# Loading the first 512 rows of x in four quarters on two queues, and moving the gate row's product to another PSUM bank

## The chip, the core and the metric

The kernel runs on one core of one Trainium2 chip. The metric is the device time of one execution in microseconds (us), as the median of several executions. All executions told here are of the fast state, except where the text says otherwise. Every execution also has a profile span (first to last instruction), about 1.3 us shorter than its time; a position in a trace is counted in us from the start of that span.

Words used below: SBUF and PSUM are the two memories in which this kernel keeps its tiles. In it TensorE writes its products to banks of PSUM (`PS<-` in the views), and DVE (the vector engine) or ACT (the scalar engine) copies them to SBUF (`XT<-PS`). SP and ACT issue the DMA transfers; a transfer "lands" at the moment that the profile gives as its landing (in before, the second half at 3.66 us, and the transpose that waited for it started at 3.71). The "pitch" is the time from the start of one matmul to the start of the next, and the "switch" the moment at which it goes from about 0.427 to 0.216 us for 512 columns. The texts call it the clock switch, and the slow pitch a slow clock; but the granted clock reads 1.00 in before from 0 to 5 us, at the slow pitch, so only the spacing of matmuls shows the switch.

## The reference, cut to what matters

```python
x = A_x                                              # 1 x 2048 x 512, bf16
g = sigmoid((x * gate_w).sum(-1, keepdims=True))     # one gate per row
a = linear_attention(x, A_wqkv, A_w_phi, A_wo)       # 32 heads of 16, two softmaxes as feature map
b = relu(x @ B_w1) @ B_w2                            # 512 -> 1376 -> 512
return g * a + (1 - g) * b
```

Only the opening concerns us: in this kernel the first 512 rows of x ("x0") are brought into SBUF with the 512 features on the partitions before `x @ w1` begins, and gate_w becomes one more column of w1.

## The kernel before: the parts that matter

All rows but the first 512 are transposed by the DMA. x0 is loaded plainly, as two halves on one queue (SP), and transposed by TensorE, 16 blocks of 128 x 128 multiplied by an identity. A block is named (dt, j): feature block dt, and j, the quarter of x0 whose rows it holds. Until x0 has landed, TensorE does filler matmuls.

```python
def loadx0(h):
    p.dma("sp", lambda e: e.dma_start(out=XS[:, 2*h:2*h+2, :], in_=xq[:, 2*h:2*h+2, :]), f"x0{h}", ev=f"x0{h}")
...
A, B = (0, 1), (2, 3)          # quarters of the first and of the second half
warm(5)                        # five fillers of 512 columns
p.early("pe")
warm(1, 384)                   # and one of 384
xtr("a0", A, (0,), 6)          # name, quarters, feature blocks, PSUM bank
xtr("a1", A, (1,), 5)
xtr("a2", A, (2,), 7, last=False)
xtr("c0", (2,), (0,), 2)       # the second half is waited for here
xtr("d0", (3,), (0,), 0)
xtr("a2", A, (3,), 7, off=2 * P)
xev("dve", "a0", A, (0,), 6)   # xev: copy from PSUM to SBUF, on DVE or ACT
xev("act", "c0", (2,), (0,), 2)
xev("dve", "d0", (3,), (0,), 0)
...
xtr("b1", B, (1, 2), 1)
xtr("b3", B, (3,), 6)
...
slab(0)                        # 8 products x0[feature block 0] @ w1; needs a0, c0, d0 and w1's first piece
```

"Slab t" is eight matmuls of 512 columns with the t-th feature block; after slab 3 come two more products, and then the gate row and two value tiles:

```python
hunit(0, 8)                    # banks 3 and 4
hunit(0, 9, "dve")
gatecol(3 + rot[0] % 3)        # bank 5: gate_w transposed by a 4-column matmul, copied into w1 by DVE
vtile(0, "dve")                # bank 2
vtile(1, "act", nextbank())    # bank 5 again
for i in range(4):
    pre(i)                     # banks 0, 1, 6, 7
```

The softmax here doesn't subtract the row's maximum and nothing guards it: scores larger than these inputs give would overflow.

## Time and profile before

| | before |
|---|---|
| median of the first three executions | 147.24 us (147.05 to 147.31) |
| the execution that was profiled | 147.74 us, span 146.4 us |
| TensorE busy | 143.2 us, 98% of the span |
| fillers, x0's transposes, slab 0 begin at | 0.39, 2.94, 4.75 us |

The lines behind this stand in the prediction. Lines of the timeline and of the chain begin with start and length in us; L numbers are lines of that kernel, so the same operation moves by one or two lines between kernels (transposes L239 before, L237 after; slabs L522 and L520; value tiles L406 and L404). A name such as `OT<-in_A_x_dram` is the load of x0 (its buffer shares memory with OT), and `PS<-ONE` a filler.

### The profile page before, as it was taken

What the parts mean: (1) busy time and instruction counts of PE and PEld (TensorE: products, weight loads), DVE (VectorE), ACT (ScalarE), POOL (GpSimd) and SP (SyncE); (2) the same over time, 40 slices, a digit from 0 to 9 for tenths busy, and PEclk for the clock granted to TensorE, in tenths of its full rate; (3) what the DMA queues carried; (4) which work ended last, traced back from release to release, by engine and by line L of the source; (5) the groups of instructions that cost most, each with busy time, mean ns of one, the idle gap of its engine ahead of it and who ended that gap; (6) DMA issues with size and microseconds to landing.
All of it is one profiled execution on the core that took longest, in us unless ns stands there. A gap on an engine that the chain in (4) does not pass through costs nothing.

```text
span 146.4 us, 2522 instructions
## 1 busy us (share of the span) xinstructions
PE 143.2 (98%) x961; PEld 73.4 (50%) x978; DVE 92.5 (63%) x158; ACT 72.8 (50%) x125; POOL 52.2 (36%) x62
## 2 busy tenths in 40 slices
PE   8999999999999999999999999999999999999994
PEld 3544664444445545545644555554444444444443
DVE  3517737777688878678698977674445555555342
ACT  3307467897778778887878862022221111111150
POOL 2040002778768678687869820300000000000000
DMA  6999993033449975335743431454243222322213
GB/s 201 283 272 206 221 182 68 0 71 72 76 85 336 149 213 76 72 72 107 44 106 74 105 72 29 83 108 116 68 100 79 72 72 57 91 72 74 72 44 106
DMA packets 45221, 16.12 MB, mean 110 GB/s; under 512 B 39352, under 2 KB 44568, under 8 KB 45208
## 3 DMA queue, kind: packets, MB, share of 16 engines
q1 hardware_dynamic: 45056, 15.92, 49.7%
q8 instruction: 8, 0.13, 0.4%
q10 hardware_dynamic: 152, 0.03, 0.1%
q14 instruction: 5, 0.04, 0.1%
HBM read 4.41 MB, written 2.10 MB: 44 GB/s over the span
## 4 chain that ended last, share of the span: by engine, by line
PE 97%; issue 1%; DVE 1%; DVEq 0%
PE PS L485 25%; PE PS L274 19%; PE PS L330 18%; PE PS L494 9%; PE PS L406 9%; PE PS L522 5%; PE PS L460 3%; PE PS L428 3%; PE PS L286 2%; PE PS L232 2%; PE PS L239 1%; PE PS L308 1%; DVE WQK L508 1%; DVE ONE L208 0%; DVEq L655 0%
## 5 line engine op out<-in xcount | busy, mean ns | idle before, releaser
L485 PE MATMUL PS<-W,HT 128*128 128x512 bf16 (+3 forms) x182 | 40.2, 366 | 0.3
L374 POOL TENSOR_TENSOR EB<-EB,SC 128x1024 bf16<-128x1024 bf16 x15 | 28.9, 1930 | 24.7 <-DVE SC L372 24.7
L350 ACT ACTIVATE EB<-PS 128x480 bf16<-128x480 f32 (+1 forms) x44 | 30.1, 756 | 14.2 <-PE PS L330 14.2
L499 ACT ACTIVATE TFA<-PS,GT 128x512 bf16<-128x512 f32 x16 | 11.0, 687 | 42.7 <-PE PS L494 36.6
L274 PE MATMUL PS<-XT,W 128*128 128x512 bf16 x124 | 30.2, 379 | 0.2
L330 PE MATMUL PS<-WQK,XT 128*128 128x480 bf16 x128 | 28.5, 366 | 0.0
L370 DVE TENSOR_REDUCE ZB<-EB 128x64 f32<-128x1024 bf16 x15 | 18.3, 1220 | 14.2 <-ACT EB L350 14.2
L508 DVE SCALAR_TENSOR_TENSOR WQK<-PS,OMG,TFA 128x512 bf16<-128x512 f32 (+2 forms) x17 | 12.2, 719 | 23.6 <-ACT TFA L499 22.4
L485 PEld LDWEIGHTS PS<-W,HT 128*128 128x128 bf16 (+1 forms) x187 | 17.0, 98 | 17.4
L260 ACT ACTIVATE HT<-PS 128x512 bf16<-128x512 f32 x35 | 20.3, 614 | 7.5 <-PE PS L522 5.6
L330 PEld LDWEIGHTS PS<-WQK,XT 128*128 128x128 bf16 x128 | 12.5, 98 | 13.6
L385 DVE TENSOR_REDUCE ZB<-EB 128x64 f32<-128x1024 bf16 x16 | 18.7, 1167 | 0.0
L274 PEld LDWEIGHTS PS<-XT,W 128*128 128x128 bf16 x128 | 12.0, 98 | 13.2
L394 POOL TENSOR_TENSOR EB<-EB,SC 128x512 bf16<-128x512 bf16 x16 | 16.9, 1059 | 1.3
L494 PE MATMUL PS<-WO,OT 128*128 128x512 bf16 x62 | 16.0, 378 | 0.1
L406 PE MATMUL PS<-WV,XT 128*128 128x512 bf16 x59 | 15.5, 379 | 0.3
L470 DVE TENSOR_TENSOR WQK<-PS,RDEN 128x512 bf16<-128x512 f32 x16 | 11.1, 691 | 0.6
L494 PEld LDWEIGHTS PS<-WO,OT 128*128 128x128 bf16 x64 | 6.1, 97 | 7.2
L416 ACT ACTIVATE VS<-PS 128x512 bf16<-128x512 f32 x14 | 8.5, 608 | 2.2 <-PE PS L406 2.2
L372 DVE RECIPROCAL SC<-ZB 128x64 f32<-128x64 f32 x16 | 8.8, 553 | 0.5
L406 PEld LDWEIGHTS PS<-WV,XT 128*128 128x128 bf16 x64 | 5.4, 97 | 5.0 <-DVE W L227 0.5
L460 PEld LDWEIGHTS PS<-KVNZ,PHQ 128*128 128x128 bf16 x128 | 6.1, 97 | 3.6
(57 smaller groups left out, 89.2 us busy)
## 6 DMA issues: line engine op xcount, KB each, us to landing
out_dram<-WQK SPq DMA_DIRECT2D x15, 128.0 KB, 1.7
W<-in_B_w_dram SPq DMA_DIRECT2D x3, 256.0 KB, 4.8
W<-in_B_w_dram SPq DMA_DIRECT2D x2, 384.0 KB, 4.8
OT<-in_A_x_dram SPq DMA_DIRECT2D x2, 256.0 KB, 2.9
WV<-in_A_wqkv_dram SPq DMA_DIRECT2D x1, 512.0 KB, 6.2
W<-in_B_w_dram SPq DMA_DIRECT2D x1, 512.0 KB, 4.1
WO<-in_A_wo_dram SPq DMA_DIRECT2D x2, 256.0 KB, 3.1
W<-in_B_w_dram SPq DMA_DIRECT2D x1, 352.0 KB, 5.7
```

Source lines behind the costliest of these rows:

```text
L260: p.op("act", lambda e: e.activation(dst, src, ACT.Relu), after=[f"h{c}_{kt}"], ev=ev)
L274: p.op("pe", lambda e, t=t: e.matmul(PS[:, bank, :], W1[:, t, kt * P:(kt + 1) * P], XT[:, t, c * 512:(c + 1) * 512], start=(t == 0), stop= ...
L330: p.op("pe", lambda e, dt=dt, which=which: e.matmul(PS[:, which, 0:DE], XT[:, dt, m * P:(m + 1) * P], WQK[:, which, dt * DE:(dt + 1) * DE] ...
L350: p.op("act", lambda e: e.activation(dst, s_, ACT.Exp, scale=scale), after=[f"qk{m}"] + busy, ev=ev)
L370: p.op("dve", lambda e: e.tensor_reduce(zk, ek, AX.X, ALU.add), after=[emk, f"cst{b}"], ev=f"zk{m}")
L374: p.op("pool" if m < NT - 1 else "dve", lambda e: e.tensor_tensor(EB[:, b, 3, :].rearrange("p (g f) -> p g f", f=DH), EB[:, b, 2, :].rearr ...
L385: p.op("dve", lambda e: e.tensor_reduce(ZB[:, b, 0:64].rearrange("p (h s) -> p h s", s=2), bass.AP(tensor=EB, offset=base, ap=[[EBS, P], [ ...
L394: p.op("pool", lambda e: e.tensor_tensor(EB[:, b, 0, :].rearrange("p (h s f) -> p h s f", h=H, s=2)[:, :, 1, :], EB[:, b, 1, :].rearrange( ...
L406: p.op("pe", lambda e, dt=dt: e.matmul(PS[:, bank, :], XT[:, dt, m * P:(m + 1) * P], WV[:, dt, :], start=(dt == 0), stop=(dt == NDT - 1)), ...
L485: p.op("pe", lambda e, kt=kt, M=M: e.matmul(PS[:, bank, 0:n], HT[0:M, kt, m * P:(m + 1) * P], W2[0:M, kt, cs], start=(kt == 0), stop=(kt = ...
L494: p.op("pe", lambda e, t=t: e.matmul(PS[:, bank, :], OT[:, t, m * P:(m + 1) * P], WO[:, t, :], start=(t == 0), stop=(t == NDT - 1)), after ...
L508: p.op("dve", lambda e: e.scalar_tensor_tensor(out=OSB[:, ob, cs], in0=PS[:, bank, 0:n], scalar=OMG[:, m:m + 1], in1=TFA[:, m % 2, cs], op ...
```

## The change

The intent: let the first quarter of x0 land earlier and be transposed at once, so that one filler can go and slab 0 starts sooner; and free the gate row's bank from the product that waited for it.

```diff
-        def loadx0(h):
-            p.dma("sp", lambda e: e.dma_start(out=XS[:, 2 * h:2 * h + 2, :], in_=xq[:, 2 * h:2 * h + 2, :]),
-                  f"x0{h}", ev=f"x0{h}")
+        def loadx0(j, eng):
+            p.dma(eng, lambda e: e.dma_start(out=XS[:, j, :], in_=xq[:, j, :]), f"x0{j}", ev=f"x0{j}")
 ...
+        for j in range(NDT):
+            loadx0(j, ("sp", "act")[j % 2])
 ...
-        warm(5)
+        warm(4)
 ...
-        xtr("a0", A, (0,), 6)
-        xtr("a1", A, (1,), 5)
-        xtr("a2", A, (2,), 7, last=False)
-        xtr("c0", (2,), (0,), 2)
-        xtr("d0", (3,), (0,), 0)
-        xtr("a2", A, (3,), 7, off=2 * P)
+        xtr("a0", ((0, 0),), 6, last=False)
+        ... the other three blocks of quarter 0, then the four of quarter 1 ...
+        xtr("c0", ((0, 2),), 2)
+        xtr("d0", ((0, 3),), 0)
         xev("dve", "a0", A, (0,), 6)
+        xev("dve", "a1", A, (1,), 5)
         xev("act", "c0", (2,), (0,), 2)
         xev("dve", "d0", (3,), (0,), 0)
 ...
-        gatecol(3 + rot[0] % 3)
+        gatecol(0)
```

More of the change, by code (lines that the diff above doesn't have):

```diff
@@ L171, in bass_gated_mix__linear_kernel_hedgehog__dense_activation_relu__prompt_kernel @@
         p.early("act")
-        for h in range(2):
-            loadx0(h)
         p.early("sp")
@@ L233, in warm, with xtr @@
                      after=["one"])
-        def xtr(nm, js, dts, bank, last=True, off=0):
-            blocks = [(dt, j) for dt in dts for j in js]
+        def xtr(nm, blocks, bank, last=True, off=0):
             for i, (dt, j) in enumerate(blocks):
@@ L240, in xtr @@
                     PS[:, bank, o:o + P], XS[:, j, dt * P:(dt + 1) * P], IDN[:, :], start=True, stop=True),
-                    after=["idn", f"x0{j // 2}"] + (free[bank] if o == 0 else []),
+                    after=["idn", f"x0{j}"] + (free[bank] if o == 0 else []),
                     ev=(f"xt{nm}" if last and i == len(blocks) - 1 else None))
@@ L528, in bass_gated_mix__linear_kernel_hedgehog__dense_activation_relu__prompt_kernel @@
         A, B = (0, 1), (2, 3)
-        warm(5)
+        warm(4)
         p.early("pe")
         warm(1, 384)
-        xtr("a0", A, (0,), 6)
-        xtr("a1", A, (1,), 5)
-        xtr("a2", A, (2,), 7, last=False)
-        xtr("c0", (2,), (0,), 2)
-        xtr("d0", (3,), (0,), 0)
-        xtr("a2", A, (3,), 7, off=2 * P)
+        xtr("a0", ((0, 0),), 6, last=False)
+        xtr("a1", ((1, 0),), 5, last=False)
+        xtr("a2", ((2, 0),), 7, last=False)
+        xtr("a2", ((3, 0),), 7, last=False, off=2 * P)
+        xtr("a0", ((0, 1),), 6, off=P)
+        xtr("a1", ((1, 1),), 5, off=P)
+        xtr("a2", ((2, 1),), 7, last=False, off=P)
+        xtr("a2", ((3, 1),), 7, off=3 * P)
+        xtr("c0", ((0, 2),), 2)
+        xtr("d0", ((0, 3),), 0)
         xev("dve", "a0", A, (0,), 6)
+        xev("dve", "a1", A, (1,), 5)
         xev("act", "c0", (2,), (0,), 2)
@@ L541, in bass_gated_mix__linear_kernel_hedgehog__dense_activation_relu__prompt_kernel @@
         xev("act", "a2", A, (2, 3), 7)
-        xev("dve", "a1", A, (1,), 5)
-        xtr("b1", B, (1, 2), 1)
-        xtr("b3", B, (3,), 6)
+        xtr("b1", [(dt, j) for dt in (1, 2) for j in B], 1)
+        xtr("b3", [(3, j) for j in B], 6)
         xev("act", "b1", B, (1, 2), 1)
```

## The prediction

Its sum came to 0.18 us (slab 0 sooner by 0.35 us, filled at the slow pitch) + 0.14 us (the gate row's hole) = 0.32 us, and 147.24 - 0.32 = 146.92, given as 146.9. The first quarter's 2.45 us is the author's estimate from the first half's landing and the rate in the trace; that this quarter would move ahead of the others was assumed.

> **What bounds the kernel now.** I read the page's busy shares first, then the chain of work that ended last in order of time, then the timeline of the first 16 us, then the waits of the weight loads.
>
> The page, busy times and chain by engine:
>
> ```profile
> PE 143.2 (98%) x961; PEld 73.4 (50%) x978; DVE 92.5 (63%) x158; ACT 72.8 (50%) x125; POOL 52.2 (36%) x62
> ...
> PE 97%; issue 1%; DVE 1%; DVEq 0%
> ```
>
> TensorE is busy for 98% of the span and is 97% of the chain. So only what shortens TensorE's own row moves the end: a matmul less, a hole closed, or less time at a slow clock. The chain in order of time (start, length, what) shows the opening:
>
> ```profile
> 0.39 2.64 PE PS L232 x6
> 3.02 1.93 PE PS L239 x16
> 4.96 6.49 PE PS L522 x27
> ...
> 12.52 1.73 PE PS L274 x8
> 14.25 0.01 PE PS L225
> 14.26 1.90 PE PS L406 x8
> ```
>
> L232 are filler matmuls on a column of ones, whose result nobody reads; L239 the 16 transposes of x0; L522 the first products (4 slabs of 8); L274 and L406 later products. L274 gives the normal pitch: 1.73 / 8 = 0.216 us for 512 columns. L406 takes 1.90 for as many, 0.17 too long: a hole. The fillers take 2.64 / 6 = 0.44 us each (five of 512 columns, one of 384): half speed.
>
> The timeline of the start (start, length, engine, what, idle before):
>
> ```profile
> 0.08 0.87 SPq L162 DMA_DIRECT2D OT<-in_A_x_dram  x2
> 0.39 2.64 PE L232 MATMUL PS<-ONE 128*128 128x512 bf16 x6 [0.39 <-DVE ONE L208]
> 2.91 0.56 PEld L239 LDWEIGHTS PS<-IDN,OT 128*128 128x128 bf16 x6 [0.69 <-DVE M L217]
> 2.94 2.01 PE L239 MATMUL PS<-IDN,OT 128*128 128x128 bf16 x16
> 3.71 0.98 PEld L239 LDWEIGHTS PS<-IDN,OT 128*128 128x128 bf16 x10 [0.23 <-DMA OT<-in_A_x_dram]
> 4.75 7.56 PE L522 MATMUL PS<-XT,W 128*128 128x512 bf16 x30
> 5.18 0.15 PEld L522 LDWEIGHTS PS<-XT,W 128*128 128x128 bf16 x1 [0.28 <-issue]
> 5.61 0.15 PEld L522 LDWEIGHTS PS<-XT,W 128*128 128x128 bf16 x1 [0.28 <-issue]
> 6.03 6.00 PEld L522 LDWEIGHTS PS<-XT,W 128*128 128x128 bf16 x28 [0.28 <-issue]
> ```
>
> Weight loads at 5.18, 5.61 and 6.03 are 0.43 apart; the 28 from 6.03 take 6.00, 0.21 each. So TensorE runs at half pitch until just past 6.03 us. Taking single matmuls out of the timeline, the one started at 6.03 is followed after 0.287 us; 512 columns fit into that if the first 0.147 us were at half pitch (0.427 us per 512) and the rest at full (0.213), so the switch is at about **6.18 us**.
>
> There are two holes before it. The last filler ends at about 2.84 (2.49 plus 384/512 of 0.427) and the first transpose starts at 2.94. The view puts that wait down to DVE, but the first half of x0, issued at 0.08, lands 2.7 us after issue, about 2.81: it is the transfer. The second half (issued 0.54, landing 3.1 later, 3.66) holds the seventh transpose: six end at 3.53, it starts at 3.71. So the holes are 0.10 and 0.18 us.
>
> The waits of the weight loads, whole span:
>
> ```profile
> PEld PS L239 <- DVE M L217: 0.7, 1, 0.7
> PEld PS L406 <- DVE W L227: 0.5, 1, 0.5
> PEld PS L239 <- DMA OT<-in_A_x_dram: 0.2, 1, 0.2
> ```
>
> The second is the gate row: its product goes into bank 5, DVE copies it out (L227) from 14.90, and the next product but one, vtile(1), wants bank 5. Its first matmul starts at 15.12 where the previous one, started at 14.76, would have let it start at 14.98: a **hole of 0.14 us**. After it no wait on TensorE is listed to the end; spacings one matmul too long are missing records.
>
> [...] The trace [...] shows one switch, at 6.18; that is 5.8 us after the first filler[...]. Whether the switch keeps its time when the work before it changes, no run here shows yet. The granted clock reads 1.00 throughout, so that column does not show this. [...] x0 moves at 300 to 400 GB/s from 1.5 to 2.7 us, from one queue. [...] almost all of x0's 512 KB have moved by 2.7 us, yet the second half lands at 3.66. [...]
>
> **The change, part by part.**
>
> *One filler less.* Four of 512 columns and one of 384 in place of five and one: TensorE is free at 2.84 - 0.43 = 2.41 us. The time is only won where a quarter of x0 is there to be transposed.
>
> *Quarters on two queues.* The bytes are the same. An issue took 0.40 us for a half, 0.34 for a piece the size of a quarter (the first W1 load). Now SP issues quarters 0 and 2, ACT 1 and 3. [...] I estimate 2.81 less half the 0.7 us in which 256 KB moved (256 KB at 370 GB/s), about 2.45; quarter 1 about 2.8; quarters 2 and 3 about 3.2 and 3.5, a little before 3.66, as their issues no longer queue. ACT starts its table load about half a microsecond later (two more issues); that load took 1.28 us from 1.11, and ACT's first evacuation is at 4.03, so this is hidden.
>
> *Transposes quarter by quarter.* Sixteen as before, 0.107 us each at half pitch. Of quarters 0 and 1, eight instead of six come before the wait for the second half, so only eight instead of ten remain after it. From 2.45: four to 2.88, four to 3.31, then the block of quarter 2, the block of quarter 3 at about 3.55, and six more, which end at about 3.55 + 7 x 0.107 = 4.30. Slab 0 also needs DVE to have copied a0, a1 and d0, now in that order: a0 from about 3.2 (0.43 us), a1 to 4.0, d0 (0.29) to about 4.3. And it needs the first piece of W1, which landed 3.1 us after 1.09, at 4.2. Three conditions meet at 4.2 to 4.35; allowing 0.05 for signals, slab 0 starts at about **4.40 instead of 4.75: 0.35 us sooner**.
>
> *What of it survives.* If the switch stays at 6.18, the 0.35 us are filled with half-speed matmuls: 0.35 / 0.427 = 0.82 of one, which later would have cost 0.82 x 0.216 = **0.18 us**. If the switch moved with the work, it would be 0.35.
>
> *Gate row in bank 0.* The product now waits for the second DVE relu (bank 0; it ends at about 12.6, the product is at 14.09) and vtile(1) for nobody. The next user of bank 0 is the first block of L308 at about 15.8, after DVE's copy (done by 15.1). The hole of **0.14 us** goes.
>
> Sum: 0.18 + 0.14 = 0.32 us. Nothing downstream should take it back: W1's slabs land at 6.3, 7.2 and 7.9, before their use (slab 1 from 7.2, later ones 1.7 us apart); the transposed weights of L308's second half land at 15.95 for use at 17.70. 147.24 - 0.32 = 146.92; I predict **146.9 us**.
>
> **The rivals.**
> *A. The transfers are what sets the start.* Half the bytes land no earlier [...]. For it: [...] 3.66 came long after the bytes had moved. Against it: the 0.1 and 0.18 us holes show the filler was already tuned to landings. Then slab 0 starts at 3.66 + 0.05 + 7 or 8 x 0.107, 4.5 to 4.6, worth 0.08 to 0.12, and the gate's 0.14: 147.0.
> *B. The clock moves.* If the earlier dense work brings the switch forward, all 0.35 survive: 146.75, or 146.6 with luck. [...]
> *C. The evacuations or W1 set slab 0.* DVE now does a1 before d0, where before it did d0 first. A slower DVE would hold slab 0 at 4.6: 147.05.
> *D. Nothing.* The gate's hole is replaced by the same wait at bank 0, or the shift is eaten: 147.2.
>
> **Range and chances.** The main line and A to C without the late switch lie between 146.6 and 147.1. The three runs of before spread by 0.26 us, which I add at the edges: 146.5 to 147.3. Two per cent would be 2.9 us; the whole opening up to slab 0 is 4.75 us, most of it work that stays, so faster by over 2% has a chance of 0.01; slower, 0.01; within 2%, 0.98.
>
> **What would show it.** Right: L232 with five matmuls; L239 starting near 2.45 with a short hole before the ninth or tenth; L522 starting at 4.3 to 4.5; the pitch changing at 6.1 to 6.2; eight L406 in 1.73 us with the wait on L227 gone; the end of the span 0.3 us sooner. Wrong: L239 still starting at 2.8 or later (A), the pitch changing elsewhere (B), a wait of L522 for DVE or W1 (C), a wait of L308 for L227 (D). A late switch alone would put the time above the range.

## The result, and the profile after

The changed kernel took 147.06 us (median of 6, 146.58 to 147.30) and the kernel before 147.15 us (median of 6, 146.90 to 147.65). The ratio is 0.9988, with a 95% interval of 0.9965 to 1.0012. Ratios here are the mean time of one kernel's fast runs over the mean of the other's of the same rounds, so they are not quite the ratio of the quoted medians. It is a difference of 0.2 us that the runs do not separate from zero.

The profiled spans, in contrast, differ by 0.4 us: 146.4 before, 146.0 after. The chain of work that ended last, of the changed kernel, its opening (start, length, what):

```profile
0.62 3.33 DMA OT<-in_A_x_dram
3.95 0.05 issue
4.00 0.93 PE PS L237 x7
4.92 6.48 PE PS L520 x28
...
12.27 1.73 PE PS L272 x8
13.99 0.00 PE PS L224
14.00 1.75 PE PS L404 x8
15.75 0.84 PE PS L306 x16
```

Where before the chain was TensorE from 0.39 us on, it now starts with a transfer: the fourth quarter, issued by ACT at 0.62, lands at 3.95, and seven transposes follow it. (The chain counts a matmul from the end of the one before it, so it gives 4.92 where the timeline has the start of slab 0 at 4.72.) The eight L404 take 1.75 us where L406 took 1.90: the gate row's hole is gone. L272 begins at 12.27 instead of 12.52, L306 at 15.75 where before L308 begins at 16.16: 0.25 us won by the first point, 0.41 by the second.

The timeline of the changed kernel's opening:

```profile
0.21 0.86 ACTq L162 DMA_DIRECT2D OT<-in_A_x_dram  x2
0.39 2.21 PE L231 MATMUL PS<-ONE 128*128 128x512 bf16 x5 [0.39 <-DVE ONE L207]
2.65 2.28 PE L237 MATMUL PS<-IDN,OT 128*128 128x128 bf16 x16
3.58 0.10 PEld L237 LDWEIGHTS PS<-IDN,OT 128*128 128x128 bf16 x1 [0.19 <-DMA OT<-in_A_x_dram]
3.99 0.66 PEld L237 LDWEIGHTS PS<-IDN,OT 128*128 128x128 bf16 x7 [0.31 <-DMA OT<-in_A_x_dram]
4.72 7.55 PE L520 MATMUL PS<-XT,W 128*128 128x512 bf16 x31
5.15 0.15 PEld L520 LDWEIGHTS PS<-XT,W 128*128 128x128 bf16 x1 [0.28 <-issue]
5.57 6.20 PEld L520 LDWEIGHTS PS<-XT,W 128*128 128x128 bf16 x29 [0.28 <-issue]
```

The transposes start 0.29 us sooner (2.65 for 2.94), but take 2.28 us instead of 2.01, as they wait for quarters 2 and 3. Slab 0 starts at 4.72: only 0.03 us sooner. And yet the products end 0.25 us sooner, because the weight loads are 0.43 us apart only up to 5.57; the 29 after that take 6.20 us, 0.21 each. Worked out as in the prediction, the switch to full pitch comes at 5.69 us here, against 6.17 to 6.18 before. So the account of the 0.41 us between these two traces is: 0.14 from the hole; half of 0.03 from slab 0's start; half of 0.49 from the switch. The last term is the largest, and the question is whether the change made it.

### The profile page after: what moved, and what is told of

The parts are those of the page before. It is cut to its first block, busy times and chain, and to the rows that moved or that the text cites. A ratio compares the mean times of both kernels' runs of the same rounds, so it can differ in the third digit from the quotient of the medians.

```text
span 146.0 us, 2522 instructions
## 1 busy us (share of the span) xinstructions
PE 142.6 (98%) x960; PEld 73.2 (50%) x977; DVE 92.5 (63%) x158; ACT 72.8 (50%) x125; POOL 52.1 (36%) x62
## 4 chain that ended last, share of the span: by engine, by line
PE 95%; DMA 2%; issue 1%; DVE 1%; ACTq 0%
PE PS L483 25%; PE PS L272 19%; PE PS L328 18%; PE PS L492 9%; PE PS L404 9%; PE PS L520 5%; PE PS L458 3%; PE PS L426 3%; DMA OT<-in_A_x_dram 2%; PE PS L284 2%; PE PS L306 1%; DVE WQK L506 1%; PE PS L237 1%; ACTq L162 0%; ACTq L657 0%
## 5 line engine op out<-in xcount | busy, mean ns | idle before, releaser
L272 PE MATMUL PS<-XT,W 128*128 128x512 bf16 x124 | 30.2, 379 | 0.2
L272 PEld LDWEIGHTS PS<-XT,W 128*128 128x128 bf16 x128 | 12.0, 98 | 13.2
L404 PE MATMUL PS<-WV,XT 128*128 128x512 bf16 x59 | 15.3, 378 | 0.3
L404 PEld LDWEIGHTS PS<-WV,XT 128*128 128x128 bf16 x64 | 5.4, 97 | 4.8
```

The lines of the kernel that those rows point to most:

```text
L272: p.op("pe", lambda e, t=t: e.matmul(PS[:, bank, :], W1[:, t, kt * P:(kt + 1) * P], XT[:, t, c * 512:(c + 1) * 512], start=(t == 0), stop= ...
L404: p.op("pe", lambda e, dt=dt: e.matmul(PS[:, bank, :], XT[:, dt, m * P:(m + 1) * P], WV[:, dt, :], start=(dt == 0), stop=(dt == NDT - 1)), ...
```

## The experiments

Twelve runs. The theory (T) after the result: from slab 0 on, TensorE has no slack, so its last matmul starts at a constant, plus slab 0's start, plus half of the time by which the pitch switches after slab 0, plus any hole; and when it switches is a draw of each execution. The rival (R): the change itself brings the switch forward. The experiments then ask what sets slab 0's start.

**a. The kernel before, once more** (no edit).

> The kernel before, unchanged, against itself: the ratio shows the noise. Theory (T): the end of TensorE's row is a constant plus half the start of slab 0 plus half the time of the clock switch plus the gate row's hole, and the switch is a draw of each execution that the kernel does not decide. Then this profile has slab 0 at 4.7 to 4.8, the hole of 0.14, and a switch anywhere from 5.5 to 6.5 us, and its last matmul starts at 138.62 + half of slab 0's start + half of the switch + 0.14, within 0.03. Rival (R): the change itself brought the switch from 6.18 to 5.69. Then this profile switches at 6.18 within 0.05. Ratio 1.000 in both, interval about 0.002 wide.

Measured: ratio 1.0006 (0.9973 to 1.0039) against itself, so this is what the noise does. The profiled execution took 147.03 us. Its timeline:

```profile
2.89 1.45 PE L239 MATMUL PS<-IDN,OT 128*128 128x128 bf16 x16
4.72 4.86 PEld L522 LDWEIGHTS PS<-XT,W 128*128 128x128 bf16 x24 [0.56 <-DMA W<-in_B_w_dram]
4.73 5.14 PE L522 MATMUL PS<-XT,W 128*128 128x512 bf16 x23 [0.39 <-DMA W<-in_B_w_dram]
```

No weight load of a slab is 0.43 us from the next here: the switch came among the transposes, at 3.14 us by their spacing. That refutes R (6.18 expected) and is also outside the range I gave for T. Slab 0 still starts at 4.73, but what it waits for is now w1's first piece. My formula had to be mended: a switch before slab 0 costs nothing more, so the term is half of the larger of zero and switch minus slab 0. With that, both executions of this kernel fit: 147.74 - 147.03 is 0.71 us, and half of 6.17 - 4.75 is 0.71 us. The same program differs by more between two executions than the change is worth.

**b. Only the gate row's bank.**

```diff
-        gatecol(3 + rot[0] % 3)
+        gatecol(0)
```

> Only the gate row's product moved to bank 0; x0 as before. T and R: the hole of 0.14 us at the first matmul of vtile(1) is gone, slab 0 at 4.75, time less by 0.14 us, ratio 0.9990. T: the switch is a draw again (5.5 to 6.5). R: the switch stays at 6.18, as the opening is that of before. A third theory (the hole comes back at the first block of L308, which wants bank 0): ratio 1.000 and a wait there.

Measured: ratio 0.9997 (0.9966 to 1.0029). In the chain of this run:

```profile
13.86 1.75 PE PS L406 x8
15.61 0.84 PE PS L308 x16
```

Eight products in 1.75 us, and no wait at L308: the hole of 0.14 us is gone and did not come back. The time cannot show 0.14 us; the trace does. The switch was at 5.35, slab 0 at 4.77.

**c. Only the quarters** (against the changed kernel).

```diff
-        gatecol(0)
+        gatecol(3 + rot[0] % 3)
```

> Only the quarters, one filler fewer; the gate row's product in bank 5 as before, so the hole of 0.14 us stays. T: slab 0 at 4.65 to 4.8 because the last quarter lands near 3.95, so half of about 0.03 us is won: ratio 0.9995 to 1.000, and the switch is a draw. R: the switch is at 5.69 within 0.05, which alone wins 0.25 us: ratio 0.998.

Measured: ratio 0.9984 (0.9953 to 1.0015). The hole stands in the chain again:

```profile
13.67 1.90 PE PS L404 x8
```

Slab 0 started at 4.49, sooner than I expected, since the last quarter landed at 3.73 this time. The switch was at 5.25, so R's 5.69 did not hold either.

**d, k. The changed kernel twice more** (no edit).

> The changed kernel again. T: 0.14 us from the hole and about 0.02 from slab 0, ratio 0.9989; the last quarter lands after 3.8, later than the second half of before (3.66); the switch a draw. R: switch at 5.69 again and ratio 0.997 to 0.9975.

> The changed kernel once more, beside the two above on one chip. T: slab 0 0.75 to 0.78 after the last quarter; the switch anywhere from 3.1 to 6.6; last matmul at 138.62 plus slab 0's start plus half of what the switch comes after it. Ratio to before 0.998 to 0.9995, and the same as the two above within the interval. Rival (the profile of the changed kernel shows its usual switch): 5.69 to 5.97 again.

Measured: ratios 0.9991 (0.9959 to 1.0022) and 0.9977 (0.9948 to 1.0007). The last quarter landed at 3.75 and 3.71, in d sooner than the 3.8 I had set; slab 0 at 4.51 and 4.47, 0.76 us after it in both; the switch at 5.97 and 5.37. So the 0.03 us of the first profile was a poor draw of the landing, and slab 0 is usually some 0.2 us sooner than before. One of the six executions of k took 149.10 us and counts as slow; it has no profile, and I leave its cause open.

**e. The kernel before without fillers.**

```diff
-        warm(5)
         p.early("pe")
-        warm(1, 384)
```

> The kernel before without its six filler matmuls, so TensorE's first work is the first transpose near 2.8 us. So far the switch to full pitch came at 6.17, 5.69, 3.14, 5.35, 5.25 and 5.97 us in six executions of kernels whose TensorE work starts at 0.39. Theory (T[...]): the switch now comes 2.5 us later than that range, between 5.4 and 9.0, and half of the delay beyond slab 0 is lost: time more by about 1.0 us, ratio 1.005 to 1.009. Rival (the switch is a time from the start of the execution, whatever TensorE does): switch between 3.1 and 6.5, ratio 1.000.

Measured: 149.18 us against 147.14, ratio 1.0117 (1.0067 to 1.0166), a little more than expected. In the timeline:

```profile
2.81 2.12 PE L239 MATMUL PS<-IDN,OT 128*128 128x128 bf16 x16 [2.81 <-DMA OT<-in_A_x_dram]
4.72 5.04 PE L522 MATMUL PS<-XT,W 128*128 128x512 bf16 x13
8.14 0.15 PEld L522 LDWEIGHTS PS<-XT,W 128*128 128x128 bf16 x1 [0.28 <-issue]
8.56 0.15 PEld L522 LDWEIGHTS PS<-XT,W 128*128 128x128 bf16 x1 [0.27 <-issue]
8.96 0.53 PEld L522 LDWEIGHTS PS<-XT,W 128*128 128x128 bf16 x3 [0.24 <-issue]
```

Transposes and slab 0 start where they did, but loads are still 0.4 us apart up to 8.96: the switch comes at 8.92 us. So when TensorE's own work began 2.4 us later, the switch came at 8.92 and not by 6.17 (one profile; the four executions took 148.06 to 149.23 us), and the fillers, whose products nobody reads, are worth 2 us. This also supplies the missing half of T: in these runs the switch is neither a fixed time nor free of the kernel. Work from 0.39 us on put it between 3.14 and 6.17 in twelve of the fourteen traces (the table below); work from 2.81 on, at 8.92.

**f. All four quarters on SP.**

```diff
-            loadx0(j, ("sp", "act")[j % 2])
+            loadx0(j, "sp")
```

> The changed kernel with all four quarters issued from SP. T (the last quarter lands late, at 3.73 to 3.95[...]): on one queue W1 comes behind the quarters, and the last quarter lands at 3.7 or earlier though its issue is 0.8 us later; W1's first piece is issued near 2.0 and lands near 5.0, which then holds slab 0 at 5.0. Rival (the smaller packets and the issues are what makes it late): the last quarter lands at 3.9 or later, and the second queue was a gain.

The question was whether the last quarter lands late because of w1's first piece in flight beside it (T) or because of its own packets and issues (the rival). Measured, one look: the last quarter landed at 3.87, between the two expectations, although it was issued only at 1.47; w1's first piece landed at 4.64 and slab 0 started at 4.69, not 5.0. So the second queue is worth little for x0, at most about 0.1 us by this look; it serves w1, whose first issue would else slip from 1.09 to 2.04. There was one more effect. The switch came in the hole between the ninth and the tenth transpose, somewhere from 3.44 to 3.92, and slab 1 then had to wait:

```profile
6.95 2.76 PE L520 MATMUL PS<-XT,W 128*128 128x512 bf16 x12 [0.37 <-DMA W<-in_B_w_dram]
```

TensorE's spacing there is 0.53 us too long. The piece waited for, w1's third, was issued at 2.89 here and landed at 6.91. In a, h and l, which also switched before slab 0, it was issued at 1.94 and landed at 5.74 to 6.04, and slab 1 waited for nothing. So it is w1 queued behind x0 that costs this, and not the early switch alone.

**g. w1 held back until x0 is in.**

```diff
         p.early("sp")
+        p.wait("sp", ["x02", "x03"])
         loadw1(0, 0, 4 * P, "a")
```

> The changed kernel, but SP issues W1's first piece only when quarters 2 and 3 have landed[...]. T: the last quarter lands at 3.4 to 3.6. Rival [...]: it lands at 3.7 to 3.95 as in the two runs of the changed kernel. In both W1 lands near 6.5 and slab 0 starts there, so the kernel is some 1.0 us slower if the switch comes after it, and up to 2 if it had come before.

The same question, with no piece of w1 in flight beside x0 (its first issue was at 3.71). Measured, one look: 149.61 us. The last quarter landed at 3.64, again between the expectations: with w1's first piece issued at about 1.09 us it landed at 3.95, 3.73, 3.75, 3.79, 3.75 and 3.71 in six executions (mean 3.78), so w1 beside it may cost about 0.1 us and no more is shown by a single look. Slab 0 waited for w1 until 5.83, TensorE was idle for 1.4 us, and the switch came at 9.27. The time is 2.5 us above the median of before, more than the 1 to 2 us expected. That the idling put the switch off is not shown by one look.

**h. The sixth filler put back into the changed kernel.**

```diff
-        warm(4)
+        warm(5)
```

> The changed kernel with the sixth filler put back: the first transpose then starts at 2.82 to 2.95 instead of 2.6. T: slab 0 is set by the last quarter's landing and starts 0.76 to 0.80 us after it (4.5 to 4.7), as without the filler, so taking the filler out was worth nothing: ratio to before 0.9985 to 0.9995, the same as the changed kernel's. Rival (the filler and the early first quarter count): slab 0 0.1 us or more later after the landing of the last quarter, that is over 0.87.

Measured: ratio 0.9975 (0.9934 to 1.0017), transposes from 2.81. The last quarter landed at 3.79 and slab 0 started at 4.54, but the switch had come at 3.20 and slab 0 waited for w1's first piece (landed 4.50). So the 0.75 us between them proves nothing here, and the run says only that putting the filler back costs no time that can be seen.

**i, l. Halves on one queue, reordered** (the kernel before, `gatecol(0)`, and two lines moved; l is the same kernel again).

```diff
         xtr("a2", A, (2,), 7, last=False)
+        xtr("a2", A, (3,), 7, off=2 * P)
         xtr("c0", (2,), (0,), 2)
         xtr("d0", (3,), (0,), 0)
-        xtr("a2", A, (3,), 7, off=2 * P)
         xev("dve", "a0", A, (0,), 6)
+        xev("dve", "a1", A, (1,), 5)
         xev("act", "c0", (2,), (0,), 2)
         xev("dve", "d0", (3,), (0,), 0)
         xev("act", "a2", A, (2, 3), 7)
-        xev("dve", "a1", A, (1,), 5)
```

> The kernel before with x0 in halves on one queue and six fillers, with two edits: the gate row's product in bank 0, and all eight transposes of the first half before the first of the second half (six in before), a1 copied before d0. In before and in the copies slab 0 started 1.07 to 1.17 us after the landing of the second half (3.56 to 3.68), and in the quartered kernels 0.75 to 0.77 after the last quarter (3.73 to 3.95). Theory (T: the last byte of x0 and the number of transposes after it set slab 0, not the size of the pieces): slab 0 at the landing plus 0.045 plus 8 x 0.107, 0.90 in all, that is 4.45 to 4.6, as in the quartered kernels; time as theirs, ratio 0.9975 to 0.999. Rival (loading by quarters is what wins): slab 0 at 4.7 or later. If the clock switches before slab 0, W1's first piece or the copies set slab 0 and the run does not tell.

> The reordered halves once more, as the version that would beat both. T: the saving over before is the gate row's hole, 0.14 us, plus half to all of 0.15 to 0.2 us of slab 0, so 0.2 to 0.35 us: ratio 0.9976 to 0.9987; slab 0 at 4.5 to 4.65; last matmul at 138.62 plus slab 0's start plus half of what the switch comes after it. Rival (the 0.9972 of the first time was a lucky set of switches and the true saving is the gate's hole alone): ratio 0.999 and slab 0 at 4.7 or later.

Measured: ratios 0.9972 (0.9949 to 0.9995) and 0.9982 (0.9946 to 1.0017); medians 146.72 and 146.83 us. The timeline of i:

```profile
0.08 0.87 SPq L162 DMA_DIRECT2D OT<-in_A_x_dram  x2
2.92 1.71 PE L239 MATMUL PS<-IDN,OT 128*128 128x128 bf16 x16
4.57 1.67 PE L522 MATMUL PS<-XT,W 128*128 128x512 bf16 x7
```

Eight transposes of the first half cover the wait: all 16 run without a hole in 1.71 us, against 2.01 before. Slab 0 starts at 4.57 in i, 0.95 us after the second half's landing at 3.62, and at 4.44 in l, 0.89 after 3.55. In both the pitch switched before slab 0 (4.33 and 3.72), so the last step was shortened a little; in i it switched during the fourteenth transpose, so the saving there is nearly all due to the order. (At the slow pitch throughout they would have ended at 4.58, an estimate from their starts.) The ninth transpose now starts at 3.73, when the second half has already landed. So the last landing no longer holds TensorE up, and slab 0 is set by the first half's landing and the row of 16 transposes after it. The quarters are not needed for most of the earlier slab 0; with the slow pitch up to slab 0 they stand at 4.47 to 4.51 in c, d and k, up to 0.1 us sooner than i, which single profiles do not settle. Beside k in the same rounds i cannot be told from the changed kernel (0.9972 and 0.9977); it is the one whose interval lies below 1, in one of two tries, and it does with fewer transfers.

**j. Quarters carried through:** all of quarter 2 before the first block of quarter 3, six fillers.

```diff
-        warm(4)
+        warm(5)
 ...
         xtr("c0", ((0, 2),), 2)
+        xtr("b1", ((1, 2),), 1, last=False)
+        xtr("b1", ((2, 2),), 1, last=False, off=2 * P)
+        xtr("b3", ((3, 2),), 4, last=False)
         xtr("d0", ((0, 3),), 0)
+        ... the other three blocks of quarter 3 ...
```

The two b3 blocks use bank 4 here, and banks 4 and 6 change places in the slabs.

> The quartered kernel with six fillers and the idea carried through: all four transposes of quarter 2 before the first of quarter 3, so four instead of seven remain after the last landing (the two b3 blocks move to bank 4, the slab order of banks follows). T (slab 0 also needs d0: one transpose, 0.29 to its end, a DVE copy of 0.29, signals, 0.70 to 0.76 together): slab 0 still 0.70 to 0.76 after the last quarter, nothing won over the quartered kernel. Rival (the remaining transposes set it): 0.045 + 4 x 0.107 = 0.47 after, so slab 0 near 4.3 and 0.15 us faster if the clock is still slow.

Measured: ratio 1.0007 (0.9979 to 1.0035). Slab 0 started at 4.83, 1.08 us after the last quarter (3.75). That is neither expectation. Two views show why, the chain and then DVE's timeline around 4.4 us:

```profile
3.01 1.71 PE PS L237 x16
4.72 0.11 issue
4.83 6.37 PE PS L520 x27
```

```profile
4.44 0.29 DVE L247 CAST XT<-PS 128x128 bf16<-128x128 f32 x1
```

The 16 transposes ran without a hole, so block d0 was the thirteenth, at 4.09, and its copy on DVE took from 4.44 to 4.73. DVE had been idle for 0.10 us before it, so the copy waited for the block and not for the copy ahead of it. Slab 0 needs that copy. So fewer transposes after the last landing win nothing if d0, which still has to be copied, runs later for it. The rival's 0.47 us after the landing is refuted; T's 0.70 to 0.76 holds counted from d0's start (4.09 to 4.83 is 0.74), and missed from the landing because d0 did not start there. One thing is mixed in: j has the sixth filler, so its transposes start at 2.81 instead of about 2.6. Without it d0 and slab 0 could have come up to 0.2 us sooner, near 4.62 (an estimate from these starts), which would still not beat the 4.47 to 4.51 of c, d and k.

**All traces together.** Last matmul of the profiled execution, in us, with what the rule above is made of. "x0" is when its last piece landed.

| run | x0 | slab 0 | switch | holes after | last matmul | its time |
|---|---|---|---|---|---|---|
| before | 3.66 | 4.75 | 6.17 | 0.14 | 144.23 | 147.74 |
| a | 3.56 | 4.73 | 3.14 | 0.14 | 143.51 | 147.03 |
| e | 3.64 | 4.72 | 8.92 | 0.14 | 145.58 | 149.23 |
| b | 3.68 | 4.77 | 5.35 | 0 | 143.68 | 147.17 |
| after | 3.95 | 4.72 | 5.69 | 0 | 143.82 | 147.30 |
| d | 3.75 | 4.51 | 5.97 | 0 | 143.86 | 147.33 |
| k | 3.71 | 4.47 | 5.37 | 0 | 143.54 | 147.01 |
| c | 3.73 | 4.49 | 5.25 | 0.14 | 143.65 | 147.12 |
| h | 3.79 | 4.54 | 3.20 | 0 | 143.18 | 146.64 |
| j | 3.75 | 4.83 | 5.64 | 0 | 143.83 | 147.29 |
| f | 3.87 | 4.69 | 3.44 to 3.92 | 0.53 | 143.86 | 147.34 |
| g | 3.64 | 5.83 | 9.27 | 0 | 146.14 | 149.61 |
| i | 3.62 | 4.57 | 4.33 | 0 | 143.19 | 146.71 |
| l | 3.55 | 4.44 | 3.72 | 0 | 143.05 | 146.56 |

Taking from the last matmul slab 0, the holes, and half of what the switch comes after slab 0 leaves 138.59 to 138.64 us in all fourteen. So nothing downstream gives back or adds: whatever the opening wins or loses arrives at the end. The switch is worked out from the one matmul whose spacing lies between the slow and the fast pitch; in j it falls between two matmuls, and in f it fell in a hole and can only be bounded. In the twelve traces other than e and g it came 2.75 to 5.78 us after TensorE's first filler.

## Why the prediction was right or wrong

The measured 147.06 lies in the range, and the class is right. By its steps:

- **The gate's hole: right, with its size.** It is in the traces of before, a, c and e at 0.14 us and in none of the ten traces with bank 0; no wait replaced it (rival D's form of it is refuted).
- **Slab 0 0.35 us sooner: right in direction, too large.** The mean of before, b and e is 4.75 (a was held by w1); that of after, c, d and k, the four with the change's opening, is 4.55: 0.20 us. The mis-sized term is the landing of "quarters 2 and 3 about 3.2 and 3.5". The profile of after has 3.54 and 3.95, and the six kernels on two queues with w1 beside them have a mean of 3.78 for the last one, against 3.62 for the second half in six executions on one queue (before, a, b, e, i, l). With the split the first piece landed sooner, at 2.45 to 2.51 (I had 2.45) instead of 2.67 to 2.81, and the last one 0.16 later. The count after it was right: 0.045 + 7 x 0.107 = 0.79, measured 0.75 to 0.77.
- **Rival A: right that the last landing decides.** Its argument, that 3.66 came long after the bytes had moved, is not what the traces show, if their packets are counted (the halves move in packets of 2 KB, the quarters and w1's first piece in packets of 1 KB). Of the 256 packets of x0 in before, 229 had ended by 2.70, but the last one ended only at 3.34, beside w1's first packets, which began at 2.66. The landing at 3.66 is 0.32 us after that.
- **Rival C: a tie.** In after, c, d and k slab 0 follows the last transpose by one pitch of 0.107 us, so TensorE did not wait for DVE. Yet d0's copy ended 0.10 to 0.11 us before slab 0, as in j, where slab 0 waited for it.
- **"Quarters" as the cause of the gain: not needed.** What gains is to have more transposes to do before the last piece: six in before, nine in the quartered kernel, eight in run i, which has most of the gain with halves. The filler's removal let the transposes start at 2.6, but they then wait for quarter 2 or 3. That it won nothing is argued from this; h, which was to show it, was decided by w1 instead.
- **"If the switch stays at 6.18": wrong as a premise.** It is a draw: 3.14 and 6.17 for one kernel, 5.69, 5.97 and 5.37 for the other. When it comes after slab 0, half of an earlier slab 0 survives, as predicted; when it comes before, what slab 0 wins by other means survives whole, but w1's first piece may be what it waits for (a, h). Rival B put the switch in the hands of the change, and that is not shown: of the two profiles that started this, 0.24 of 0.41 us was luck.
- **The spread.** I added the 0.26 us of three runs at the edges. It is larger: 146.50 to 147.70 in eleven executions of before. A switch between 3.14 and 6.17 accounts for up to half of 6.17 - 4.75, that is 0.7 us of these 1.2 (an estimate from the table). The rest would need slab 0 itself to move in executions that have no profile. And 0.26 added at both edges of 146.6 to 147.1 is 146.3 to 147.4, not the range I gave.
- **Slips that changed nothing.** 2.49 + 0.32 is 2.81, not 2.84, so the first hole is 0.13 us and TensorE would be free at 2.38. The first transpose started 0.13 to 0.14 us after its piece had landed (before, after, c, d, k), where I had it start at the landing; the wait for the last piece hid this.

What the change is worth, then: 0.14 plus half to all of 0.20, 0.24 to 0.34 us, where I had 0.32 from a wrong split. The three ratios of the changed kernel, 0.9988, 0.9991 and 0.9977, have a mean of 0.9985, or 0.22 us. Each of the three intervals contains 1.

**Open:** why the last piece of quartered x0 lands later. The packets split the 0.16 us: the last one of the fourth quarter ended at 3.32 to 3.56 in the six kernels (mean 3.40), that of the second half at 3.23 to 3.34 in the six on one queue (mean 3.29), and the landing followed after 0.38 to 0.39 us instead of 0.32 to 0.34. So about 0.1 is later movement, for which w1's packets beside it are the candidate (in g, without them, the last packet ended at 3.28, on one look), and 0.06 a later signal without a cause. Open too: the one execution of 149.10 us; and whether the filler that was taken out makes late switches more frequent, which would need many more executions.

## What to carry to other kernels

When one engine is busy for the whole span (TensorE for 98% here), write its end as a sum of a few terms of the opening and check that sum on several traces; here it held within 0.05 us over fourteen, where the executions of one kernel spread over 1.2 us. Before splitting a load, look at which landing the work really waits for. Here, with the DMA busy share at 0.93 from 2 to 3 us in before, the first piece landed at 2.45 to 2.51 instead of 2.67 to 2.81, but the last, for which the work waited, at 3.78 instead of 3.62 in the mean. So first put all the work that needs only the early pieces ahead of that wait. And take more than one profile before explaining a difference that is smaller than the spread of the runs.
